# Decode attention for two problems on one core: a semaphore of its own for each problem's x, a four-row mask product, and x asked for at once

## The chip, the cores and the metric

The kernel runs on one core of one Trainium2 chip. The metric is device microseconds of that core. Every time of a whole kernel is a median of several executions. Times inside a kernel are those of its one profiled execution.

## The reference, cut to what matters

Two independent problems, A and B, of the same shape are computed and their outputs are joined.

```python
B, Sq, D = 2, 1, 576
Hq, Hkv, Sk, Dh = 32, 16, 16384, 128
W = min(4096, max(256, Sk // 4))                 # 4096: only the last 4096 keys are used
q = (x @ wq).reshape(B, Sq, Hq, Dh)              # wq: 576 x 4096
k = repeat(k_cache[:, :, Sk - W:, :], 2); v = repeat(v_cache[:, :, Sk - W:, :], 2)
scores = einsum("bhqd,bhkd->bhqk", q, k) * Dh ** -0.5
o = einsum("bhqk,bhkd->bhqd", softmax(scores), v)
out = o.reshape(B, Sq, Hq * Dh) @ wo             # wo: 4096 x 576
```

Everything is bf16. There is one query per batch row, so the work is reading: wq and wo are 4.7 MB each per problem, the used keys 33.6 MB and the used values 33.6 MB per problem. Together 153.1 MB come from HBM.

## The kernel before

The loads run on the queue of SyncE (SP), in one fixed order: wq of A, wq of B, K0, K1, K2, K3, V0, K4, V1, K5 and so on. A K or V load is one "slab" of 4 MB: four heads of one batch row. Slabs live in a ring of four slots; wq of A and B lie in slots 0 to 2 at the start, K0 has slot 3. So K0 can be asked for at once, but K1 (slot 0) must wait until the q matmuls have read wq of A, and K2 and K3 until they have read wq of B:

```python
first_deps = {0: [q_done[0]], 1: [q_done[0], q_done[1]], 2: [q_done[1]], 3: []}
...
slot_of[key] = (n_slot + 3) % NSLOT              # K0: slot 3, K1: 0, K2: 1, K3: 2, V0: 3, K4: 0
...
deps = [last_reader[prior[-1]]] if prior else first_deps[r]   # what the load of a slot waits for
```

For q, x (2 rows of 576 per problem) is brought into the form that the tensor engine wants. The rows of both problems land in a zeroed 32-row buffer, one DVE product with a mask spreads them, and eight transposes (of 32 x 288 each, in 32x32 blocks) turn them. One semaphore covers all four x loads, and both q matmul groups wait for the last transpose:

```python
def f_x(e):                                       # four small loads on ACT's queue, one semaphore
    for P in range(NPROB):
        for h in range(2):
            last = e.dma_start(xz[4*P+2*h:4*P+2*h+2, P*D:(P+1)*D], probs[P][0][:, 0, :]).then_inc(x_sem, 16)
    return last
p_zx  = pool(lambda e: e.memset(xz.bitcast(FP32), 0.0), [], "zero_x")       # after four other POOL operations
x_dma = dma_op("act", x_sem, 2 * NPROB, f_x, [p_zx], "x")
d_xs  = dve(... tensor_tensor(xs, xz, hmask, mult) ..., [x_dma, d_hm], "xs")        # 32 x 2304
d_xT  = dve(f_xT, [d_xs], "xT")                   # eight block transposes of 32 x 288
...                                               # six small masks follow on DVE
q_done[P] = pe(f_q, [wq_dma[P], d_xT], "q%d" % P) # 36 matmuls per problem
```

After q come its evacuation (ACT), a transpose, and the matrices Z (POOL). From then on, for each K slab, DVE transposes two halves (4.4 us each), PE makes scores, and a softmax and the product with V follow. A slot comes free when its reader is done.

## Time and profile before

364.45 us, median of 3 runs (364.19 to 365.74). The span of the profile is 363.5 us.

| what | value | view |
|---|---|---|
| busy: PE, DVE, ACT | 64%, 60%, 13% | page, part 1 |
| load queue q1 | 153.10 MB, 98.4% of 16 engines' span | page, part 3 |
| loads, 50 to 140 us and 140 to 340 us | 436 and 430 GB/s | windows |
| loads, 30 to 50 us | 393 GB/s | windows |

The page's load queues (queue: packets, MB, share of the time of 16 DMA engines):

```profile
q1 hardware_dynamic: 6196, 153.10, 98.4%
q8 instruction: 8, 0.13, 0.1%
...
q10 hardware_dynamic: 20, 0.01, 0.0%
...
```

q1 is SP's queue with all the big loads, q10 is ACT's with x and an output; q8, with eight packets, matters in the experiment fetch_early. The kernel is bound by q1. At the 432 GB/s that 50 to 340 us show, 153.1 MB take 354.4 us (worked out), so engine work counts only where it makes a load late.

Windows of the kernel before (stretch in us, its length; busy us of PE, PEld, DVE, ACT, POOL; granted PE clock, share of the DMA engines, GB/s):

```profile
30.00:50.00 20.00, 15.47 (x68) 2.42 (x25) 8.77 (x2) 3.47 (x10) 1.04 (x4) 0.85 0.94 393
33.50:36.50 3.00, 3.00 (x16) 0.31 (x4) 1.46 (x1) 0.00 (x0) 0.00 (x0) 1.00 0.55 175
50.00:140.00 90.00, 62.71 (x308) 14.17 (x206) 66.22 (x33) 10.02 (x16) 5.87 (x22) 0.90 1.01 436
140.00:340.00 200.00, 134.27 (x758) 33.97 (x571) 124.47 (x84) 30.45 (x49) 10.40 (x37) 0.83 1.00 430
```

The last two numbers of a line tell it: loading is steady from 50 us on, and weak around 35 us.

Timeline of the kernel before, first 50 us, picked lines (start us, duration us, engine, line, operation, out<-in, number; in brackets the idle time before it and what ended it; SPq and ACTq are the load requests):

```profile
2.44 0.82 ACTq L179 DMA_DIRECT2D xt<-in_A_x_dram  x2
3.29 0.58 ACTq L179 DMA_DIRECT2D xt<-in_B_x_dram  x2
...
15.79 2.54 DVE L217 TENSOR_TENSOR xt<-xt,hmask 32x2304 bf16<-32x2304 bf16 x1 [14.21 <-DMA xt<-in_B_x_dram]
18.37 5.59 DVE L224 STREAM_TRANSPOSE pT<-xt 32x288 bf16<-32x288 bf16 x8
...
24.10 0.58 PE L271 MATMUL ot<-ring,pT 128*32 128x512 bf16 x1 [24.10 <-DVE pT L224]
...
33.43 8.96 SPq L370 DMA_DIRECT2D ring<-in_A_k_cache_dram  x3
...
35.04 4.45 DVE L425 STREAM_TRANSPOSE xt<-ring 128x4096 f32<-128x4096 f32 x1 [9.63 <-DMA ring<-in_A_k_cache_dram]
...
46.71 0.58 PE L451 MATMUL st<-xt,zq 128*128 128x512 bf16 x1 [1.46 <-POOL zq L417]
...
```

x is asked for at 2.4 to 3.9 us, and the product starts at 15.79, when the x of B has landed. q of A starts at 24.10. K1 is asked for at 33.43 (the first of the three in that line), and K0 has landed at 35.02, so that DVE starts on it at 35.04. So K1 is asked for only 1.6 us before K0 has landed, and nothing else stands in the load queue then: that is the weak stretch around 35 us.

### The profile page before, as it was taken

The numbers are of one execution on the slowest core, as the hardware profiler recorded it, in microseconds if no ns is written. First come the engines' busy times: TensorE is split into PE (matmuls) and PEld (weight loads), VectorE is DVE, ScalarE is ACT, GpSimd is POOL, SyncE is SP. The second block draws the span as 40 slices with busy tenths as digits, with TensorE's granted clock in tenths as the row PEclk, the third lists the DMA queues.
The fourth block names the chain that finished last, engine by engine and source line by source line (L and its number), as shares of the span: only waits on it lengthen the run. The fifth ranks groups of instructions, "written<-read, shape, count | busy, mean of one in ns | idle before, by whom it ended". The sixth has DMA issues, their size and how long they took to land.

```text
span 363.5 us, 2622 instructions
## 1 busy us (share of the span) xinstructions
PE 233.1 (64%) x1292; PEld 56.3 (15%) x927; DVE 218.2 (60%) x149; ACT 46.0 (13%) x78; POOL 22.4 (6%) x83
## 2 busy tenths in 40 slices
PE   0039688737675675567586676654676875666865
PEld 0001111101211121112122121101112121112222
DVE  0271829857758585583918594941926776765532
ACT  1000300050005000500005000500005000501400
POOL 4010010110001000100010001000010000000000
PEclk9999979978988796888888989968588798869899
DMA  8998999999999999999999999999999999999995
GB/s 325 455 425 353 462 404 456 404 462 404 462 404 456 407 455 398 438 443 422 443 422 438 425 425 423 448 411 454 411 451 414 447 415 436 442 418 440 411 415 239
DMA packets 6227, 153.26 MB, mean 422 GB/s; under 512 B 700, under 2 KB 840, under 8 KB 1224
## 3 DMA queue, kind: packets, MB, share of 16 engines
q1 hardware_dynamic: 6196, 153.10, 98.4%
q8 instruction: 8, 0.13, 0.1%
q14 instruction: 3, 0.02, 0.0%
q10 hardware_dynamic: 20, 0.01, 0.0%
HBM read 153.10 MB, written 0.00 MB: 421 GB/s over the span
## 4 chain that ended last, share of the span: by engine, by line
DVE 34%; DMA 32%; PE 22%; issue 8%; ACT 2%; POOL 1%; ACTq 0%; SPq 0%; DVEq 0%; POOLq 0%
DVE xt L425 20%; DMA ring<-in_B_k_cache_dram 16%; DMA ring<-in_B_v_cache_dram 9%; PE st L256 7%; PE st L451 7%; PE pj L256 4%; DMA xt<-in_B_x_dram 3%; DMA wob<-in_B_wo_dram 3%; DVE oR L558 3%; DVE pT L498 2%; DVE mx L459 2%; DVE tmp L551 2%; DVE pT L224 2%; ACT pR L489 1%; PE pj L610 1%
## 5 line engine op out<-in xcount | busy, mean ns | idle before, releaser
L451 PE MATMUL st<-xt,zq 128*128 128x512 bf16 x256 | 121.1, 473 | 83.4 <-DVE xt L425 82.0
L425 DVE STREAM_TRANSPOSE xt<-ring 128x4096 f32<-128x4096 f32 x32 | 141.4, 4426 | 25.9 <-DMA ring<-in_A_k_cache_dram 9.6
L256 PE MATMUL st<-xt,zq 128*128 128x512 bf16 x256 | 119.9, 468 | 0.0
L489 ACT ACTIVATE pR<-st,bias 128x512 bf16<-128x512 f32 x32 | 40.1, 1421 | 211.4 <-DVE bias L482 211.4
L451 PEld LDWEIGHTS st<-xt,zq 128*128 128x128 bf16 x256 | 28.8, 112 | 203.9 <-issue 105.7
L528 PE MATMUL ot<-ring,pT 128*32 128x512 bf16 x512 | 31.4, 385 | 7.4 <-DMA ring<-in_B_v_cache_dram 7.4
L482 DVE SCALAR_TENSOR_TENSOR bias<-vmask,tb,offm 128x4 f32<-128x4 f32 x8 | 1.8, 224 | 38.7 <-PE tb L479 38.7
L271 PE MATMUL ot<-ring,pT 128*32 128x512 bf16 x18 | 7.3, 404 | 24.1 <-DVE pT L224 24.1
L512 DVE TENSOR_REDUCE ssum<-tb 128x2 f32<-128x8 f32 x8 | 1.3, 161 | 35.1 <-PE tb L509 35.1
L498 DVE STREAM_TRANSPOSE pT<-pR 128x2048 bf16<-128x2048 bf16 x8 | 18.4, 2302 | 0.7 <-ACT pR L489 0.7
L417 POOL TENSOR_TENSOR zq<-qs,bmask 128x64 bf16<-128x64 bf16 x32 | 8.6, 292 | 162.2 <-PE st L256 142.2
L551 DVE SCALAR_TENSOR_TENSOR tmp<-ot,rsb,dmask 128x512 f32<-128x512 f32 x16 | 11.5, 719 | 8.9 <-PE ot L528 8.9
L558 DVE TENSOR_REDUCE oR<-tmp 128x128 f32<-128x512 f32 x15 | 15.6, 1040 | 0.5
L528 PEld LDWEIGHTS ot<-ring,pT 128*32 128x32 bf16 x512 | 12.1, 97 | 22.3 <-DMA ring<-in_B_v_cache_dram 10.0
L610 PE MATMUL pj<-wob,oM 128*2 128x288 bf16 x48 | 13.0, 304 | 0.0
L256 PE MATMUL pj<-wob,oM 128*2 128x288 bf16 x48 | 12.9, 303 | 0.0
L256 PE MATMUL pj<-ring,pT 128*32 128x512 bf16 x36 | 11.5, 404 | 0.0
L217 DVE TENSOR_TENSOR xt<-xt,hmask 32x2304 bf16<-32x2304 bf16 x1 | 2.5, 2545 | 14.2 <-DMA xt<-in_B_x_dram 14.2
L459 DVE TENSOR_REDUCE mx<-st 128x2 f32<-128x1024 f32 x8 | 9.7, 1214 | 0.1
L489 ACT ACTIVATION_READ_ACCUMULATOR pR<-st,bias 128x1 f32 x32 | 9.1, 284 | 0.0
L271 PEld LDWEIGHTS ot<-ring,pT 128*32 128x32 bf16 x18 | 1.8, 100 | 38.2 <-issue 38.2
L256 PE MATMUL st<-ring,pT 128*32 128x512 bf16 x18 | 7.1, 393 | 0.0
(67 smaller groups left out, 73.2 us busy)
## 6 DMA issues: line engine op xcount, KB each, us to landing
ring<-in_A_k_cache_dram SPq DMA_DIRECT2D x8, 4096.0 KB, 21.2
ring<-in_A_v_cache_dram SPq DMA_DIRECT2D x8, 4096.0 KB, 26.7
ring<-in_B_k_cache_dram SPq DMA_DIRECT2D x8, 4096.0 KB, 26.5
ring<-in_B_v_cache_dram SPq DMA_DIRECT2D x7, 4096.0 KB, 31.0
ring<-in_A_wq_dram SPq DMA_DIRECT2D x1, 4608.0 KB, 13.7
ring<-in_B_wq_dram SPq DMA_DIRECT2D x1, 4608.0 KB, 24.0
wob<-in_A_wo_dram SPq DMA_DIRECT2D x2, 2304.0 KB, 27.1
wob<-in_B_wo_dram SPq DMA_DIRECT2D x1, 2304.0 KB, 27.5
```

The lines of the kernel that those rows point to most:

```text
L256: return e.add_instruction(mybir.InstMatmult(name=nc.get_next_instruction_name(), engine=mybir.EngineType.PE, ins=[e.lower_ap(mv_), e.lowe ...
L271: last = e.matmul(QB[c], wt, mv_, start=first, stop=True, skip_group_check=True)
L417: last = e.tensor_tensor(dst, src, msk, ALU.mult)
L425: Xop[(t, jh)] = dve(lambda e: e.transpose(xt[:, jh, :].bitcast(FP32).rearrange("p (kp x kt) -> p x kp kt", kp=2, kt=2), ring[:, r, jh * H ...
L451: last = e.matmul(ob, wt, mv_, start=first, stop=True, skip_group_check=True)
L459: ch[(G, "max")] = dve(lambda e: e.tensor_reduce(mx[:], st[:, :].rearrange("p (x t) -> p t x", t=2), AX.X, ALU.max), [Sop[(2 * G + 1, 1)]] ...
L489: last = e.activation(pR[:].rearrange("p (x k) -> p k x", k=4)[:, kv, :], st[:, :].rearrange("p (x t) -> p t x", t=2)[:, kv % 2, :], ACTF.Exp,
L498: pT_op[G] = dve(lambda e: e.transpose(pT[:, v, :].rearrange("p (w j q) -> p j w q", w=4, q=8), pR[:].rearrange("p (j w q) -> p j w q", w= ...
L528: last = e.matmul(OTB[32 * c:32 * c + 32, :], pT[:, v, base + 32 * c:base + 32 * c + 32], ring[:, r, jj * 128:(jj + 4) * 128], start=rd == ...
L551: evac_op[i] = dve(lambda e: e.scalar_tensor_tensor(tv, o, rsb[:, v, b:b + 1], dm, ALU.mult, ALU.mult), deps, "ev%d" % i)
L558: ch[(G, "red%d" % b)] = dve(lambda e: e.tensor_reduce(oR[:, b, :], tmp[:].rearrange("p (j d) -> p d j", j=4), AX.X, ALU.add), [evac_op[i] ...
L610: last = e.matmul(PJ[h], oM[:, j, :], mv_, start=start and j == 0, stop=True, skip_group_check=True)
```

## The change

It is meant to make q of A wait for x of A alone and to get x earlier: x is asked for as ACT's first operation, into four rows that need no zeroing; each problem has its own semaphore, product (4 x 1152) and four transposes; the six masks move between the two problems.

```diff
-        x_sem = sem("xload")
+        x_sem = [sem("xload%d" % P) for P in range(NPROB)]
-        def f_x(e):
-            last = None
-            for P in range(NPROB):
+        x_dma = []
+        for P in range(NPROB):
+            def f_x(e, P=P):
                 for h in range(2):
-                    last = e.dma_start(xz[4 * P + 2 * h:...], ...).then_inc(x_sem, 16)
+                    last = e.dma_start(x4[2 * h:2 * h + 2, P, :], probs[P][0][:, 0, :]).then_inc(x_sem[P], 16)
+                return last
+            x_dma.append(dma_op("act", x_sem[P], 2, f_x, [], "x%d" % P))
-        p_zx = pool(lambda e: e.memset(xz.bitcast(FP32), 0.0), [], "zero_x")
-        x_dma = dma_op("act", x_sem, 2 * NPROB, f_x, [p_zx], "x")
+        p_zxU = pool(lambda e: e.memset(pTf[:, 0:XW].bitcast(FP32), 0.0), [], "zero_xU")
+        p_zx = pool(lambda e: e.memset(xs.bitcast(FP32), 0.0), [], "zero_x")
-        d_xs = dve(... 32 x 2304 ..., [x_dma, d_hm], "xs")
-        d_xT = dve(f_xT, [d_xs], "xT")                   # 8 transposes
+        d_xT = []
+        def turn_x(P):
+            d_xs = dve(... 4 x 1152 ..., [x_dma[P], d_hm, p_zx], "xs%d" % P)
+            d_xT.append(dve(f_xT, [d_xs, p_zxU], "xT%d" % P))   # 4 transposes
+        turn_x(0)
         ... six masks ...
+        turn_x(1)
-            q_done[P] = pe(f_q, [wq_dma[P], d_xT], "q%d" % P)
+            q_done[P] = pe(f_q, [wq_dma[P], d_xT[P]], "q%d" % P)
```

(The view xU gets 40 columns so that x of B can be placed at column 4.)

More of the change, by code (lines that the diff above doesn't have):

```diff
@@ L120, in build_kernel @@
         bsel = sb("bsel", [128, 2], FP32)
-        hmask = sb("hmask", [32, 2], FP32)
+        hmask = sb("hmask", [4, 2], FP32)
         mx = sb("mx", [128, 2], FP32)
@@ L146, in build_kernel @@
         pTf = pT[:].rearrange("p v f -> p (v f)")
-        XW = NPROB * NU * 32
+        XW = NPROB * NU * 40
         xU = pTf[:, 0:XW].rearrange("p (g u w) -> p g u w", g=NPROB, u=NU)
@@ L150, in build_kernel @@
         assert XW + 512 <= 2 * 2048
-        xz = xt[0:32, 0, 0:NPROB * D]
+        x4 = xt[0:4, 0, 0:NPROB * D].rearrange("p (g i) -> p g i", g=NPROB)
         xs = xt[0:32, 1, 0:NPROB * 2 * D]
@@ L173, in dma_op @@
             return op
-        def f_x(e):
-            last = None
-            for P in range(NPROB):
+        x_dma = []
+        for P in range(NPROB):
+            def f_x(e, P=P):
                 for h in range(2):
-                    last = e.dma_start(xz[4 * P + 2 * h:4 * P + 2 * h + 2, P * D:(P + 1) * D], probs[P][0][:, 0, :]).then_inc(x_sem, 16)
-            return last
+                    last = e.dma_start(x4[2 * h:2 * h + 2, P, :], probs[P][0][:, 0, :]).then_inc(x_sem[P], 16)
+                return last
+            x_dma.append(dma_op("act", x_sem[P], 2, f_x, [], "x%d" % P))
         wq_dma = {}
@@ L215, in mask, with f_xT @@
             return dve(lambda e: e.tensor_reduce(dst, view, axes, ALU.add), [p_ident_f], tag)
-        d_hm = mask(hmask[:, 0:2], ident_f[0:32, 0:32].rearrange("p (g t b) -> p t g b", g=8, t=2), AX.XY, "hmask")
-        d_xs = dve(lambda e: e.tensor_tensor(xs.rearrange("p (i t) -> p i t", t=2),
-                                             xz.unsqueeze(2).broadcast_to([32, NPROB * D, 2]),
-                                             hmask[:, 0:2].unsqueeze(1).broadcast_to([32, NPROB * D, 2]), ALU.mult), [x_dma, d_hm], "xs")
-        def f_xT(e):
-            for P in range(NPROB):
+        d_hm = mask(hmask[:], ident_f[0:4, 0:4].rearrange("p (t b) -> p t b", t=2), AX.X, "hmask")
+        d_xT = []
+        def turn_x(P):
+            d_xs = dve(lambda e, P=P: e.tensor_tensor(xs[0:4, P * 2 * D:(P + 1) * 2 * D].rearrange("p (i t) -> p i t", t=2),
+                                                      x4[:, P, :].unsqueeze(2).broadcast_to([4, D, 2]),
+                                                      hmask[:, 0:2].unsqueeze(1).broadcast_to([4, D, 2]), ALU.mult),
+                       [x_dma[P], d_hm, p_zx], "xs%d" % P)
+            def f_xT(e, P=P):
                 for k in range(4):
-                    last = e.transpose(xU[32 * k:32 * k + 32, P, :, :],
+                    last = e.transpose(xU[32 * k:32 * k + 32, P, :, 4 * P:4 * P + 32],
                                        xs[:, P * 2 * D:(P + 1) * 2 * D].rearrange("p (c t) -> p t c", t=NU)[:, :, 32 * k:32 * k + 32])
-            return last
-        d_xT = dve(f_xT, [d_xs], "xT")
+                return last
+            d_xT.append(dve(f_xT, [d_xs, p_zxU], "xT%d" % P))
+        turn_x(0)
         d_bm = mask(bmask[:, 0:4], ident_f[:].rearrange("p (a i) -> p a i", a=4), AX.X, "bmask")
@@ L267, in f_q @@
                     for c in range(4):
-                        wt, mv_ = xU[:, P, u, :], wqv[P][:, u, c * 512:(c + 1) * 512]
+                        wt, mv_ = xU[:, P, u, 0:32], wqv[P][:, u, c * 512:(c + 1) * 512]
                         first = P == 0 and u == 0
@@ L423, in make_X @@
             r = slot_of[("K", t)]
-            deps = [stream_dma[("K", t)][0][2], Sop[(t - 1, jh)] if t >= 1 else d_xT]
+            deps = [stream_dma[("K", t)][0][2], Sop[(t - 1, jh)] if t >= 1 else d_xT[1]]
             Xop[(t, jh)] = dve(lambda e: e.transpose(
```

## The prediction

> **What bounds the kernel now.** The loads. The page's queue table gives q1 98.4% of 16 engines' span, 153.1 MB. Windows over the trace give 436 GB/s from 50 to 140 us and 430 from 140 to 340 us, 432 together. The Trainium skill, "DMA: Bandwidth & Descriptors", Specifications, states a fabric ceiling of 435 GB/s; the trace agrees. At 432 GB/s the 153.1 MB need 354.4 us of the 363.5 us span (worked out), so at most 9 us can be won, of which start and tail keep about 4. DVE (60%) and PE (64%) have slack.
>
> **Where the loads run dry.** wq of A and B and K0 (13.6 MB) are asked for at once. K1 waits for q of A, K2 and K3 for q of B (ring slots). In the timeline x is asked for at 2.4 to 3.6 us and lands at 15.8 (the wait before the mask product). Then the mask product takes 2.54 us, eight block transposes 5.59, q of A runs from 24.1 to about 32.6, q of B to 41.2. So K1 is asked for just as K0 runs out. Windows: 33.5 to 36.5 us move 175 GB/s, 30 to 40 us 367, 39.5 to 50 us about 399. Against 432 that loses 0.65 MB plus 0.33 MB: 1.5 + 0.8 = 2.3 us.
>
> **What the change does.** x of A is asked for at about 0.8 us, without the memset before it, so should land no later than wq of A (14.5). The same page, Queues, rings and completion order, says that an engine takes turns between queues by packets; that 2 KB took 12.2 us behind wq fits waiting for a turn, so I don't count on x within 3 us. The product per problem is half as wide: 1.3 us (estimate, half of 2.54); four transposes 2.8 us (0.69 each). Added: a 128x360 memset on POOL (estimate 0.4 us) and a doubled one on xt, done before 5 us. The masks' 2.2 us of DVE now come before x of B, hidden under wq of B (lands 25.3).
>
> Expected: q of A starts at 14.6 (latest 19), ends near 23; q of B runs from 25.4 to 33.6; K1 is asked for near 23 (was 32.6), K2 near 33.6 (was 41); the first score matmul at about 39.5 (was 46.7), held by q's evacuations and the transpose of K0 (35.04 + 4.4). Compute moves 7 to 8 us earlier, but the loads soon stop it: K2 can't land before about 52.
>
> **How much is on the critical path.** Only the recovered loading. After 50 us the load queue never runs dry (21 to 31 us from issue to landing for 10 us loads), so earlier compute buys no later bytes; DVE and PE in the chain of waits are slot releases, not the limit. Gain 2.0 us of the 2.3 found: 364.45 becomes 362.4 us, 0.6% faster; 80% range 361.0 to 363.9. Faster by over 2%: 3%; within: 96%; slower: 1%.
>
> **What would show it.** Right: the rate of 30 to 50 us rises from 393 to about 430 GB/s; the dip at 33.5 to 36.5 is gone; 50 to 340 us stays at 430 to 434; DVE waits longer for K; the last 25 us look the same, 2 us earlier. Wrong: x of A lands after 19 us; the first score is not near 39.5; the rate dips elsewhere.
>
> **What would make it wrong.** The rate after 50 us is set by slot timing, not the ceiling (up to 4 us more); the dip at 35 us is bookkeeping of large packets (nothing won); the tail absorbs the gain.

## The result, and the profile after

363.13 us, median of 6 runs (363.01 to 363.35), against 364.56 for the kernel before in the same rounds (364.19 to 365.74). The ratio is 0.9957, 95% interval 0.9942 to 0.9972: 1.43 us, within 2%. Ratios here are the mean time of one kernel's fast runs over that of the other's fast runs of the same rounds, so they are not quite the ratio of the medians. A second set of rounds (last experiment) gave 363.23 against 365.01, ratio 0.9949.

The same views after the change. Windows:

```profile
30.00:50.00 20.00, 14.05 (x58) 2.90 (x30) 14.04 (x4) 3.47 (x10) 1.59 (x6) 0.83 1.02 441
33.50:36.50 3.00, 0.54 (x4) 0.28 (x4) 1.73 (x1) 2.29 (x8) 0.00 (x0) 0.86 0.99 426
50.00:140.00 90.00, 59.56 (x290) 13.57 (x198) 62.83 (x33) 9.97 (x16) 5.33 (x20) 0.88 1.00 431
140.00:340.00 200.00, 137.60 (x770) 34.65 (x576) 124.28 (x84) 30.18 (x49) 10.41 (x37) 0.82 1.00 431
```

Timeline:

```profile
0.80 0.81 ACTq L179 DMA_DIRECT2D xt<-in_A_x_dram  x2
1.64 0.58 ACTq L179 DMA_DIRECT2D xt<-in_B_x_dram  x2
...
8.25 1.34 DVE L222 TENSOR_TENSOR xt<-xt,hmask 4x1152 bf16<-4x1152 bf16 x1 [6.70 <-DMA xt<-in_A_x_dram]
9.63 2.78 DVE L229 STREAM_TRANSPOSE pT<-xt 32x288 bf16<-32x288 bf16 x4
...
14.20 0.61 PE L279 MATMUL ot<-ring,pT 128*32 128x512 bf16 x1 [14.20 <-DMA ring<-in_A_wq_dram]
...
24.31 9.92 SPq L378 DMA_DIRECT2D ring<-in_A_k_cache_dram  x3
...
34.77 4.45 DVE L433 STREAM_TRANSPOSE xt<-ring 128x4096 f32<-128x4096 f32 x1 [16.72 <-DMA ring<-in_A_k_cache_dram]
...
39.27 0.61 PE L459 MATMUL st<-xt,zq 128*128 128x512 bf16 x1 [2.03 <-DVE xt L433]
...
```

q of A now waits only for wq of A (14.20), K1 is asked for 9.1 us earlier (24.31), and the first score matmul starts 7.4 us earlier (39.27). The dip at 35 us is gone, and the rate later is what it was. The 7.4 us of earlier compute are spent in waiting. Waits of DVE's transposes for K, before and after (engine, line, what it waited for: us in total, times, longest):

```profile
DVE xt L425 <- DMA ring<-in_A_k_cache_dram: 9.6, 1, 9.6
DVE xt L425 <- DMA ring<-in_B_k_cache_dram: 7.5, 2, 5.7
```

```profile
DVE xt L433 <- DMA ring<-in_A_k_cache_dram: 18.8, 2, 16.7
DVE xt L433 <- DMA ring<-in_B_k_cache_dram: 7.9, 2, 5.0
```

**A finer clock than windows.** A big load is moved by 16 DMA engines, and each adds one to the load's semaphore when its share has landed. The trace has the time of each of the 16. I call the first of them "first" and the last "last": first tells how far an undisturbed engine is; last minus first is the lag of the slowest one, and the kernel waits for last.

| landing, us (first / last) | before | after |
|---|---|---|
| K0 | 34.47 / 35.02 | 34.26 / 34.74 |
| K1 | 45.55 / 45.75 | 43.97 / 44.47 |
| K2 | 55.26 / 55.91 | 53.69 / 55.57 |
| V14 | 343.65 / 345.93 | 342.13 / 344.15 |
| last part of wo | 359.16 / 361.38 | 357.62 / 359.62 |

From K1 to K2 first moves 9.71 us before and 9.72 after: that is a 4 MB load at the full rate, 432 GB/s. From K0 to K1 it moves 11.08 before and 9.71 after. So 1.37 us are won there, 0.21 already lay in K0, and the difference of first then stays at 1.5 to 1.6 us to the end: it is there when K1 lands, before 46 us, and it is kept. The slowest engine's lag differs at the end by another 0.2 (2.2 against 2.0), which makes 1.76 us in the profiled runs. Only the 1.37 us belong to the change as far as is shown. The 0.21 and the 0.2 are not far above what two profiles of one kernel differ by: the changed kernel, profiled once more (after_again), had K0's first landing at 34.37 instead of 34.26 and a lag of 2.12 instead of 2.00 at the end.

### The profile page after: what moved, and what is told of

It is laid out like the page before. It is cut to its first block, busy times and chain, and to the rows that moved or that the text cites. A ratio compares the mean times of both kernels' runs of the same rounds, so it can differ in the third digit from the quotient of the medians.

```text
span 361.8 us, 2625 instructions
## 1 busy us (share of the span) xinstructions
PE 240.2 (66%) x1292; PEld 57.2 (16%) x927; DVE 218.7 (60%) x150; ACT 46.0 (13%) x78; POOL 24.3 (7%) x84
## 4 chain that ended last, share of the span: by engine, by line
DMA 48%; DVE 26%; PE 16%; issue 8%; ACT 1%; POOL 0%; SPq 0%
DMA ring<-in_B_k_cache_dram 17%; DVE xt L433 16%; DMA ring<-in_A_k_cache_dram 13%; DMA ring<-in_B_v_cache_dram 9%; DMA ring<-in_B_wq_dram 7%; PE st L264 5%; PE st L459 5%; DMA wob<-in_B_wo_dram 3%; PE pj L264 2%; DVE oR L566 2%; DVE mx L467 2%; DVE pT L506 2%; DVE tmp L559 2%; PE ot L536 2%; PE pj L618 1%
## 5 line engine op out<-in xcount | busy, mean ns | idle before, releaser
L459 PE MATMUL st<-xt,zq 128*128 128x512 bf16 x256 | 124.1, 485 | 86.1 <-DVE xt L433 86.1
L264 PE MATMUL st<-xt,zq 128*128 128x512 bf16 x256 | 122.7, 479 | 0.0
L536 PE MATMUL ot<-ring,pT 128*32 128x512 bf16 x512 | 32.6, 396 | 3.9 <-DMA ring<-in_B_v_cache_dram 3.9
L425 POOL TENSOR_TENSOR zq<-qs,bmask 128x64 bf16<-128x64 bf16 x32 | 8.7, 293 | 168.1 <-PE st L264 145.8
L279 PE MATMUL ot<-ring,pT 128*32 128x512 bf16 x18 | 7.6, 421 | 15.0 <-DMA ring<-in_A_wq_dram 14.2
L536 PEld LDWEIGHTS ot<-ring,pT 128*32 128x32 bf16 x512 | 12.4, 99 | 19.6 <-DMA ring<-in_B_v_cache_dram 5.5
L222 DVE TENSOR_TENSOR xt<-xt,hmask 4x1152 bf16<-4x1152 bf16 x2 | 2.7, 1349 | 6.7 <-DMA xt<-in_A_x_dram 6.7
L469 POOL TENSOR_TENSOR mv<-mx,v 128x2 f32<-128x2 f32 x8 | 1.6, 195 | 75.8 <-DVE mx L467 75.8
```

The source lines that it names most:

```text
L264: return e.add_instruction(mybir.InstMatmult(name=nc.get_next_instruction_name(), engine=mybir.EngineType.PE, ins=[e.lower_ap(mv_), e.lowe ...
L279: last = e.matmul(QB[c], wt, mv_, start=first, stop=True, skip_group_check=True)
L425: last = e.tensor_tensor(dst, src, msk, ALU.mult)
L459: last = e.matmul(ob, wt, mv_, start=first, stop=True, skip_group_check=True)
L536: last = e.matmul(OTB[32 * c:32 * c + 32, :], pT[:, v, base + 32 * c:base + 32 * c + 32], ring[:, r, jj * 128:(jj + 4) * 128], start=rd == ...
```

## The experiments

Theory L: only a late request for a load costs time. Once K1 (and every later load) is asked for early enough, when x came, how q was split, and when compute began make no difference. Rival S: splitting x by problem wins by itself. Rival X: asking for x at once wins. Rival C: compute starting 7 us earlier wins. All experiments edit the changed kernel, except x_early_whole, which edits the kernel before. In the rounds of the experiments the kernel before read 365.0 to 365.4 us.

### x_early_whole: the early request alone

```diff
+        p_zx = pool(lambda e: e.memset(xz.bitcast(FP32), 0.0), [], "zero_x")      # first on POOL
         p_ones_f = pool(...)
         ...
-        p_zx = pool(lambda e: e.memset(xz.bitcast(FP32), 0.0), [], "zero_x")
         x_dma = dma_op("act", x_sem, 2 * NPROB, f_x, [p_zx], "x")
```

> The kernel before with one thing changed: the memset of x's buffer is the first POOL instruction, so that x of both problems is asked for at about 1.4 us instead of 2.4. Product and transposes stay whole. Theory L (only loading recovered at the start counts): x lands near 9, product and transposes take 8.2 us, q of A starts near 17 and K1 is asked for near 26, about 9 us before K0 lands; the whole gain is there, 363.0 to 363.4 us, 0.3 to 0.5% under before. Rival S (splitting x by problem and the narrow product are what wins): under a third of the gain, 364.1 us or more.

Measured: 364.75 us (364.21 to 365.36), ratio 0.9989 (0.9974 to 1.0005): no clear gain. The expectation of theory L was missed, at its first step. x was asked for 1 us earlier and landed only 0.3 us earlier. Its timeline:

```profile
1.40 0.81 ACTq L179 DMA_DIRECT2D xt<-in_A_x_dram  x2
2.24 0.68 ACTq L179 DMA_DIRECT2D xt<-in_B_x_dram  x2
...
15.48 2.55 DVE L217 TENSOR_TENSOR xt<-xt,hmask 32x2304 bf16<-32x2304 bf16 x1 [13.40 <-DMA xt<-in_B_x_dram]
...
33.44 8.95 SPq L370 DMA_DIRECT2D ring<-in_A_k_cache_dram  x3
...
```

Why x took so long is in the packets of ACT's queue in the kernel before. This is their list up to the landing. Each x load has two rows, which go to two DMA engines, so each group is: start us of the two packets, bytes of each. A line is one load, its data and then its count:

```
 6.80  6.98   1152     8.21  8.39   4
 9.58  9.75   1152    10.98 11.16   4
12.35 12.53   1152    13.76 13.93   4
13.77 13.95   1152    15.18 15.35   4
```

The first two lines are the two loads of A, the last two those of B. On each engine a packet starts every 1.4 us, until the last data packet, which follows its predecessor at once. A packet of wq, 36,864 bytes for one partition, takes 1.36 us, so one of them lies between; that is read from the spacing, since the trace does not name a packet's engine. Every x row costs two turns, one for its 1,152 bytes and one for the 4 bytes that count up the semaphore. The Trainium skill ("DMA: Bandwidth & Descriptors", Queues, rings and completion order) says that each engine takes turns between queues packet by packet, with some 9 to 17 descriptors to a packet as typical; the turns are seen here, and here a turn is one packet of 36,864 bytes. So x of A lands near 11 us and x of B near 15.5. This agrees with the next experiment. In the changed kernel, where x is asked for at 0.80 us, the first load of A goes out at 1.72, before the first packet of wq (1.82), and pays no turn; x of A lands at 8.2. The theory's condition (K1 asked for early enough) was not met in this run, since q still waited for x of B and then for 8.2 us of DVE work: K1 was asked for at 33.44, as before.

### x_late_split: the split without the early request

```diff
-            x_dma.append(dma_op("act", x_sem[P], 2, f_x, [], "x%d" % P))
+            x_dma.append(dma_op("act", x_sem[P], 2, f_x, [p_zxU], "x%d" % P))
```

> The changed kernel, but x is asked for only after the memset of xU (at about 2.3 us, as before). Theory L: x of A lands near 15 to 16 as before, product and four transposes take 4.1 us, q of A starts near 20 and K1 is asked for near 28.5, 6 us before K0 lands: whole gain, 363.0 to 363.4 us. Rival X (asking at once is what wins, also because the first loads go faster): the gain is lost, 364.1 us or more.

Measured: 363.05 us (363.04 to 363.17), ratio 0.9941 (0.9928 to 0.9953): the whole gain. x of A was asked for at 2.27 us and landed at 11.3, not at 15 to 16; K1 was asked for at 25.77, 8.5 us before K0 lands. Rival X falls.

### joint_wait: the early request and the narrow products, without the separate wait

```diff
-            q_done[P] = pe(f_q, [wq_dma[P], d_xT[P]], "q%d" % P)
+            q_done[P] = pe(f_q, [wq_dma[P], d_xT[1]], "q%d" % P)
```

> The changed kernel, but q of A waits for the transposed x of B as well (asked for at once, narrow products, no separate wait). x of B is ready near 18 us, q of A starts near 18.2 and K1 is asked for near 27, 7.5 us before K0 lands. Theory L with a needed lead of about 2.4 to 3 us: nothing lost, 363.0 to 363.4 us. If the separate wait by itself is what wins: over 364 us.

Measured: 363.22 us (363.10 to 363.44), ratio 0.9944: the whole gain again, with K1 asked for at 28.53. Semaphores and products are still split by problem here; only the wait of q of A is not. Rival S falls as a necessity: the separate wait is one of several ways to be early enough.

### compute_late_7 and compute_late_15: loads early, compute late

```diff
+        for _ in range(11):                      # 24 in compute_late_15
+            q_ev[3] = act(lambda e: e.activation(qrow[96:128, :], QB[3], ACTF.Copy), [q_done[1], q_ev[3]], "qe_again")
```

> The changed kernel with eleven repeats of the last evacuation of q: about 7 us more on ACT before q is turned, so the first score matmul is near 46.5 us as in the kernel before, while K1, K2 and K3 are asked for as early as in the changed kernel. Theory L: 363.0 to 363.4 us, nothing lost. Rival C: 364.3 us or more.

Measured: 363.24 us (363.18 to 363.37), ratio 0.9945. The first score matmul was at 45.85 us, within 1 us of the kernel before, and nothing was lost. Rival C falls.

```profile
45.85 0.58 PE L461 MATMUL st<-xt,zq 128*128 128x512 bf16 x1 [1.47 <-POOL zq L427]
```

> The changed kernel with 24 instead of 11 repeats of q's last evacuation: compute starts 8 us later again, first score near 54.5 us. With 11 repeats the tightest request of the early stretch was K5, asked for at 87.5 us with 5.2 us of queued loading left. Theory L: now it is asked for near 95.5 us, 2.8 us after the queue ran out; with a needed lead of 2.3 us 5.1 us are lost, once: 367.5 to 369.3 us. Rival C (every us of compute delay costs alike): the first 7 us cost nothing, so no consistent forecast but about 363.3 if compute never matters at all.

Measured: 368.65 us (368.16 to 369.73), ratio 1.0097: 5.4 us over compute_late_7. Its requests for K4, V1, K5 and V2 in the timeline:

```profile
68.20 0.54 SPq L380 DMA_DIRECT2D ring<-in_A_k_cache_dram  x1
78.13 0.54 SPq L380 DMA_DIRECT2D ring<-in_A_v_cache_dram  x1
95.58 0.54 SPq L380 DMA_DIRECT2D ring<-in_A_k_cache_dram  x1
101.56 0.54 SPq L380 DMA_DIRECT2D ring<-in_A_v_cache_dram  x1
```

K5 was asked for at 95.58, while V1 (the load ahead of it) had first landed at 92.53. K5's first landing was 14.97 us after V1's instead of 9.71: 5.26 us lost in that one place, as forecast. So some 7 us of compute delay are free early on; of the 8 us after them 5.3 were lost.

### k1_after_qB: compute early, K1 late

```diff
-        first_deps = {0: [q_done[0]], 1: [q_done[0], q_done[1]], 2: [q_done[1]], 3: []}
+        first_deps = {0: [q_done[1]], 1: [q_done[0], q_done[1]], 2: [q_done[1]], 3: []}
```

> The changed kernel, but K1 waits for q of B (near 33.1 us) instead of q of A; compute starts as early as in the changed kernel. Theory L: the dip at 35 us is back, the loads from K2 on land 1.5 to 2.2 us later than in the changed kernel, and the time is 364.6 to 365.3 us, no better than before. Rival C (starting compute 7 us earlier is what wins): 363.1 us, gain kept. If the dip was only bookkeeping of big packets: 363.1 us as well.

Measured: 364.33 us (364.18 to 364.39), 0.3 us under the expected range. K1 was asked for at 33.31; K1's first landing was 10.90 us after K0's, 1.19 more than 9.71, and 1.2 us is what the time lost against the changed kernel. So the dip is real and not bookkeeping, and compute started early is worth nothing when K1 is late. Its requests for K1 to K3, and its line for 30 to 50 us, which is back near that of before:

```profile
33.31 1.83 SPq L378 DMA_DIRECT2D ring<-in_A_k_cache_dram  x3
...
30.00:50.00 20.00, 14.29 (x56) 2.66 (x27) 12.69 (x3) 3.46 (x10) 1.22 (x5) 0.83 0.94 400
```

### How early is early enough: k1_in_qB_5, k1_in_qB_7, k1_after_X0, k2_after_X1

For the first two, q of each problem is cut in two operations after 5 or 7 of its 9 steps, and K1 waits for the first one of B. For the others a wait on a transpose of K0 is added where loads are issued.

```diff
-        first_deps = {0: [q_done[0]], ...
+        first_deps = {0: [q_mid[1]], ...          # after 5 or 7 of the 9 steps
```
```diff
+            if key == ("K", 1): deps = deps + [Xop[(0, 0)]]      # k1_after_X0
+            if key == ("K", 2): deps = deps + [Xop[(0, 1)]]      # k2_after_X1
```

> The changed kernel, K1 waits for the first 5 of the 9 steps of q of B: asked for near 29.4 us, 5.4 us before K0 lands. From the kernel before (asked for 2.4 us ahead, about 1.5 us lost) the needed lead is about 3.9 us: nothing lost, 363.0 to 363.4 us. Rival: the loss grows evenly with any delay of K1 after 24 us: about 364.

> The changed kernel, K1 waits for the first 7 of the 9 steps of q of B: asked for near 31.1 us, 3.6 us before K0 lands. With a needed lead of 3.9 us 0.3 us are lost: 363.2 to 363.7 us. If the needed lead is only 2.3 us: 363.1 us.

> The changed kernel, K1 waits for the first transpose of K0 (done near 39.2 us), 4.4 us after K0 lands. With a needed lead of 3.9 us 8.3 us are lost: 371.4 us. With one of 2.3 us 6.7 us: 369.8 us. If compute or anything but the loads had slack to make this up, less than 5 us.

> The changed kernel, K2 (and so K3) waits for the second transpose of K0 (near 43.6 us) instead of q of B (33.1 us). K1 lands near 44.6, so the lead is about 1 us: 1.3 us (needed lead 2.3) to 2.9 us (needed lead 3.9) are lost, 364.4 to 366.0 us.

Measured: 363.20, 364.98, 370.42 and 365.10 us. The table has the requests of all these kernels that came late or near to it, and K1 of some others, sorted by lead; K and V loads that are left out had 4.6 us of lead or more and lost nothing from being late. "Lead" is how long before the first landing of the load ahead the request was made; "lost" is the distance between the two first landings, less 9.71 us.

| kernel, load | asked for at | load ahead, first landing | lead | lost | time, us |
|---|---|---|---|---|---|
| after, K1 | 24.31 | 34.26 | 9.95 | 0.00 | 363.13 |
| x_late_split, K1 | 25.77 | 34.32 | 8.55 | 0.01 | 363.05 |
| joint_wait, K1 | 28.53 | 34.28 | 5.75 | 0.00 | 363.22 |
| k1_in_qB_5, K1 | 29.88 | 34.40 | 4.52 | 0.00 | 363.20 |
| before, K2 | 41.20 | 45.55 | 4.35 | 0.00 | see its K1 |
| x_early_whole, K2 | 41.21 | 45.35 | 4.14 | 0.01 | see its K1 |
| k1_in_qB_7, K1 | 31.49 | 34.37 | 2.88 | 0.59 | 364.98 |
| k1_after_qB, K1 | 33.31 | 34.41 | 1.10 | 1.19 | 364.33 |
| before, K1 | 33.43 | 34.47 | 1.04 | 1.37 | 364.45 to 365.4 |
| x_early_whole, K1 | 33.44 | 34.21 | 0.77 | 1.43 | 364.75 |
| k2_after_X1, K2 | 43.98 | 44.07 | 0.09 | 2.22 | 365.10 |
| compute_late_15, K5 | 95.58 | 92.53 | -3.05 | 5.26 | 368.65 |
| k1_after_X0, K1 | 39.55 | 34.32 | -5.23 | 7.53 | 370.42 |

Where the lead is 1.1 us or less, lost plus lead is 2.2 to 2.4 us in every row: the request needs some 2.3 us of lead, and every us less is a us of the total. At 4.1 us and more nothing is lost. At 2.9 us it is not a sharp edge: 0.6 us are lost. The needed lead of 3.9 us that I forecast with was too large, since K1 of the kernel before was asked for at 33.43 and not at 32.6; 2.3 us was the better of the two forecasts for k1_after_X0 (369.8 forecast, 370.42 measured), neither was good for k1_in_qB_7.

**The row that doesn't fit.** k1_in_qB_7 lost 1.85 us of time with only 0.59 us lost by the first engine. The rest is in the lag of the slowest engine: its K1 landed from 44.67 to 46.19 (lag 1.5; 0.6 in k1_in_qB_5), and its V14 from 342.83 to 345.85 (lag 3.0; 1.9 in k1_in_qB_5). On the way one engine's lag went from 1.05 to 2.59 after an instruction fetch at 145.8 us (next section): the delays of the uneven restart and of the fetches add up. So an uneven restart of the 16 engines at a nearly dry queue cost more than first alone shows, in the one run of this kernel that was profiled. Why they restarted so unevenly at a lead of 2.9 us, and evenly at 1.1 us (lag of K1 0.57), no run tells.

### fetch_early: what makes one engine lag

In the runs so far the lag of the slowest engine is 0.5 to 1.0 us at K0, jumps to 1.7 to 2.5 at K2, K3 or V0, and then changes little (k1_in_qB_7, where it is 1.5 already at K1, shows its jump later). In compute_late_15 alone it goes away again: 2.52 at V1, 0.42 at K5, for which the queue had run dry. The jump follows the first of eight 16 KB packets on another queue, which the trace calls the instruction queue: the packet starts at 61.63 us and K3 (64.97) shows the jump in the kernel before, at 53.36 and K2 (53.69) in the changed one, at 67.50 and V0 (73.11) in compute_late_15. To move that packet, PE was given 200 small matmuls in its idle time before q.

```diff
+        def f_idle(e):
+            o = STT[0][:, 0:64]
+            last = e.matmul(o, ones_b[:, :], ones_b[:, 0:64], start=True, stop=True, skip_group_check=True)
+            for _ in range(199):
+                last = mm_held(e, o, ones_b[:, :], ones_b[:, 0:64], True)
+            return last
+        pe(f_idle, [p_ones_b], "idle")
```

> The changed kernel with 200 small matmuls on PE before q, in its idle time. In all runs so far the 16 KB packets of the instruction queue start at fixed places of PE's program (the first before its 129th matmul, at 53 to 62 us), and at the next landing one of the 16 engines is 1.2 to 1.5 us behind the others. Theory F (the fetch causes the lag): the first such packet now comes at 8 to 12 us, the last of the 16 increments of wq of A arrives over 1.5 us after the first (0.5 to 0.8 so far), and none of K2 or K3 shows a new jump before the next fetch near 70 us. If the lag has another cause, the jump stays at K2 or K3. Time: the largest lag at the end is much the same, 363.0 to 363.7 us.

Measured: the packet moved to 11.21 us. The lags of the 16 engines behind the first, sorted, at four landings of this run:

```
wq of A  0.0 0.12 0.14 0.14 0.19 0.22 0.23 0.29 0.3  0.31 0.32 0.37 0.38 0.44 0.44 2.0
K0       0.0 0.11 0.13 0.14 0.18 0.19 0.21 0.22 0.26 0.28 0.3  0.31 0.35 0.41 0.42 2.01
K3       0.0 0.12 0.13 0.14 0.19 0.2  0.22 0.23 0.27 0.28 0.3  0.32 0.36 0.42 0.44 2.02
V0       0.0 0.13 0.14 0.15 0.19 0.2  0.22 0.24 0.26 0.28 0.3  0.33 0.36 0.44 1.96 2.03
```

One engine is 1.6 us late at the first landing after the packet, no new lag shows at K2 or K3, and a second engine drops out at V0, after the second packet (64.75 us). So an instruction fetch of 16 KB (the packets take 0.97 to 1.13 us in the trace) delays one DMA engine by about 1.5 us, in most cases one that was not yet behind, and while the queue is full that engine never makes it up. By the last load, 7 to 11 of the 16 engines are more than 1.2 us behind the first, and the kernel waits for the slowest. The Trainium skill ("Runtime: NRT & Kernel Launch", Instruction fetch mechanics) says that instructions are fetched in 16 KiB blocks through a queue that the sequencer drives, and calls the cost mostly hidden. The 16 KB packets agree. What the fetch costs PE was not looked at; for the loads its cost is not hidden.

The time was missed: 364.59 us (364.27 to 365.70) instead of 363.0 to 363.7. The longer program needs a ninth fetch, at 348.2 us (its page counts nine packets on q8, as shown below), and after it the lag went from 1.9 (V14) to 3.4 us (last part of wo, 357.96 to 361.36): a jump of 1.5 us on top of the largest lag, so an engine must have been hit that was already behind. The profiled run is the 365.70 one: its last part of wo lands 1.74 us later than in the changed kernel, and its time is 2.69 us longer, so this tells the larger part of why that run is slow. For the other runs it is likely, not shown.

```profile
q8 instruction: 9, 0.15, 0.2%
```

### after_again: the changed kernel once more

> The changed kernel once more, unedited. The kernel before has read 365.1 to 365.4 us in the rounds of the experiments, against 364.6 in those of the changed kernel, with single runs near 364.2 and near 365.5. If the changed kernel is steady and the kernel before has two kinds of runs: 363.0 to 363.4 us again, ratio 0.994 to 0.996. If the later rounds are slower for every kernel: 363.8 us or more.

Measured: 363.23 us (363.04 to 363.49) against 365.01 (364.36 to 365.89), ratio 0.9949 (0.9935 to 0.9962). The changed kernel is steady, and the kernel before spreads over 1.5 us in both sets of rounds. The gain is 1.4 to 1.8 us. The two ranges of the kernel before would fit a fetch that sometimes hits an engine twice, but its slow runs were not profiled, so this stays open.

No version that was tried beats the changed kernel; x_late_split, joint_wait, k1_in_qB_5 and compute_late_7 equal it within 0.2 us.

## Why the prediction was right or wrong, point by point

The prediction was right: 362.4 us with 361.0 to 363.9, measured 363.13; 0.6% forecast, 0.4 to 0.5% measured.

- *The loads bound it, and 7 to 8 us of earlier compute buy nothing.* Right, and shown: compute_late_7 takes the 7 us away again and costs nothing, k1_after_qB keeps them with a late K1 and loses 1.2 us. The rate of 50 to 340 us was 432 before and 431 after. It agrees with the fabric ceiling of 435 GB/s that the prediction cited from the Trainium skill.
- *Times of the steps.* q of A at 14.20 (14.6 forecast), K1 asked for at 24.31 (23), K2 at 33.05 (33.6), first score at 39.27 (39.5), product 1.34 us (1.3), four transposes 2.78 us (2.8), the masks 1.4 us (2.2). Right within 1.3 us.
- *x lands at 15.8 and should land no later than 14.5.* The bound held (x of A at 8.2), but 15.8 was the landing of x of B, the last of four small loads that wait turn by turn. x_early_whole shows that asking 1 us earlier does not mend that.
- *2.3 us of lost loading, 1.5 + 0.8.* The mis-sized terms. The first term, the dip before K1, measured 1.37 us by first landings. The second, 0.8 us in 39.5 to 50 us, is not there: K2 followed K1 by 9.71 us before and 9.72 after. Its request had a lead of 4.35 us. The error was to read lost bytes from windows of 3 to 10 us. A K load goes in packets of 32,768 bytes, one on each of 16 engines, 0.5 MB together every 1.21 us, nearly in step, and a window's rate comes out when each packet is counted whole where it starts: of 39.5 to 50 us, 10.5 us long, that counts 128 packets, 8 for each engine, which is the 399 GB/s, while the packets' own times fill the 16 engines without a gap. It is also why 30 to 50 us show 441 GB/s after the change, more than the steady rate: 269 packets started in it.
- *K1 is asked for at about 32.6.* It was 33.43: I had worked it out from the matmuls' rate, while SP's timeline shows it.
- *The last 25 us look the same, 2 us earlier.* Right in kind: the last part of wo lands at 359.62 instead of 361.38, 1.76 us earlier.
- *Gain 2.0 us.* 1.43 and 1.78 in the two sets of rounds. By first landings the request for K1 is worth 1.37, and the rest is small beside the 1.5 us over which the runs of the kernel before spread. The sum behind the forecast counted 0.8 us that were not there; that the total still came near is in part luck, and in part the 0.3 us that were taken off.

## What to carry to other kernels

In a kernel that is bound by loading, look for the first request that is made too shortly before the load ahead of it lands (here, with loads of 4 MB, under some 2 to 4 us before). Here that request was worth its shortfall, once, and everything else that started earlier was worth nothing. Several different versions (the change, the split without the early request, the joint wait, K1 released after 5 of 9 steps of q of B) give the same 363.1 to 363.2 us because each puts that one request early enough, and the one that seemed closest to the name of the change, asking earlier alone, does not. To measure such gaps use the landing times of successive equal loads, and the first and last of the 16 engines apart; windows of a few us carried an error here as large as the effect.

## What the Trainium skill lacked or had wrong

- "DMA: Bandwidth & Descriptors", Queues, rings and completion order: it gives 9 to 17 descriptors as a typical packet between turns. Here a turn was one packet of 36,864 bytes, 1.4 us, and a small load behind such packets paid two turns per row, one for its data and one for the 4 bytes that count up its semaphore: the last of four such loads, 2.3 KB asked for at 3.6 us, landed at 15.8.
- The same page, Latency and other measured facts: it gives about 0.6 us to the first byte for this kind of queue, and no page says how far ahead the next big load must be asked for to keep the queue full. Here 2.2 to 2.4 us where the request is late, with nothing lost at 4.1 us and 0.6 us lost (1.85 us of time) at 2.9.
- "Runtime: NRT & Kernel Launch", Instruction fetch mechanics: it calls the fetch of a 16 KiB block mostly hidden. Under a full load queue each fetch put one of 16 DMA engines about 1.5 us behind, and the lag stayed to the end (1.7 to 2.2 us from the first to the last engine at the last load in most runs, 3.0 and 3.4 in the profiled runs of k1_in_qB_7 and fetch_early).
- No page has the uneven restart of the 16 engines after a nearly dry queue: 1.5 us between first and last at a lead of 2.9 us in the one profiled run of k1_in_qB_7, against 0.6 with a full queue and 0.2 to 0.6 at leads of 1.1 us and less, where the loads had not yet met an instruction fetch.
